# The first two rows of a spectral gate and token mixer: second root on ScalarE straight from the variance, first weights' low part on GpSimd, low part of row 0 in two halves

## The chip, the cores and the metric

The kernel runs on one core of a Trainium2 chip. The metric is the device time of one execution in microseconds (us). Before the change it is 366.05 us, the median of 3 runs (365.9 to 366.07).

## The reference

The input x has 2048 tokens of 512 channels. It is layer-normalised over the channels. One branch multiplies its two-dimensional Fourier transform by a filter and transforms back. The other branch normalises again, mixes over the tokens with two matrix products and a GELU between them, and goes through a SiLU. The output is x plus the product of the two.

```python
def _layernorm(x, axis=-1, eps=1e-5):
    m = jnp.mean(x, axis=axis, keepdims=True)
    v = jnp.var(x, axis=axis, keepdims=True)
    return (x - m) / jnp.sqrt(v + eps)

X = rfft2(xn) * (w_r + 1j * w_i)                       # A
s = irfft2(X, s=(S, D))
h = _layernorm(xn)                                     # B
u = gelu(einsum("bsd,sf->bdf", h, w1) + b1)            # F = 1792
y = einsum("bdf,fs->bds", u, w2) + b2
out = x + s * silu(transpose(y))                       # xn = _layernorm(x)
```

With v the variance of a token of x, the first layer norm scales by 1/sqrt(v + eps), and both together by 1/sqrt(v(1 + eps) + eps^2). So a token needs two inverse roots of the same variance.

## The kernel before, in words

**Tiling.** The 2048 tokens are 16 "rows" j of 128 tokens (one to a partition) by 512 channels. The first product accumulates over the 16 rows in PSUM: for each j, a weight tile of 128 x 128 by the row's 128 x 512. A product of two fp32 numbers is made of three products in the fp32r format: each operand is split into a high part (a rounded copy, made by `high` on ScalarE) and a low part (the number minus its high part, made by `low` on VectorE), and the products are high x high, low x high and high x low. For the weights the tiles are `w[a][0]` (high, named w1h in the trace) and `w[a][1]` (low, w1l), where a is 0 or 1 for the two halves of the columns (3 x 128 = 384 columns each in this first stage). For the data they are `hh[j]` and `hl[j]`, and the normalised row before the split is `h`; all three bear the name h in the trace. In the trace these matmuls stand under line 139, as every operation that is recorded through the helper class `Kept`.

**Order.** Nearly all instructions of the first stage are wrapped in `keep`, which fixes the order of the program on each engine's queue; the rest is ordered by the planner of the language from its costs. Each engine works its queue in order and waits at semaphores for what other engines make.

**The first rows.** To start TensorE early, rows 0 and 1 have steps of their own, which this change touches.

- `issued` (lines 449 to 452) sends the first transfers in pieces from two queues at a time: row 0 of x, the first half of the weights of row 0, row 1 of x, the second half of the weights; GpSimd's queue waits for row 0 of x (a one-column copy, line 457) and then issues more.
- TensorE first multiplies zeros (`wz`, line 443), and then twice the first high weights by themselves (lines 487 and 488).
- `stats` and `first_roots` (lines 218 to 224): mean and variance with bn_stats and bn_aggr, both sums v2 = (v + eps, v(1 + eps) + eps^2) on VectorE, both roots in one ScalarE instruction (sd), and on VectorE t = -v2/2.
- `first_scales` (lines 226 to 237): the reciprocal r0 of both roots, and one Newton step for each. The second one (index b) is done on VectorE (lines 229 and 230), as hh waits for it. The first one (index a) is done on GpSimd by four small instructions (lines 231 to 234), and then two more give q, the ratio of the two scales (`product_of_scales`, lines 240 and 241), with which `turned` (line 280) scales the small Fourier table cf for the other branch. `between` makes hh of row 0 directly on VectorE (`normed_v`, line 272, two halves of 256 channels); after it comes nb, minus mean times scale (line 237).
- `normed` (line 268) makes h on ScalarE from nb and the scale, also in two halves of 256 channels. The halves lie interleaved in the tile in blocks of 128 channels (`mirrored`).
- `low(w[0][1], ...)` is the first low part of the weights and `low(hl[0], h, hh[0])` the low part of row 0, both on VectorE, line 469.

TensorE takes for row 0, in this order, groups of 3 matmuls: first high weights x hh, second high weights x hh, first low weights x hh, first high weights x hl, second high weights x hl, second low weights x hh. After row 0 each row takes the full 18 matmuls, and on odd rows the first transform of the Fourier branch between them. Later stages (filters, the rest of the first product, the second product, the gate) are not touched.

Of the kernel before, what the change touches and what calls it, by code (L numbers as in the profile page):

```python
# [9 lines left out]
F32 = mybir.dt.float32  # L10
F32R = mybir.dt.float32r
AF = mybir.ActivationFunctionType
ALU = mybir.AluOpType
PSUM = bass.MemoryType.PSUM

P = 128
# [3 lines left out]
EPS = 1e-5  # L20
# [121 lines left out]
def spectral_mixer_kernel(tc, x, w1, b1, w2, b2, wk, we, wx, c_f, c_ft, c_d, c_i, c_g, c_h, out):  # L142
    nc = tc.nc
    V, A, G, T, SY = nc.vector, nc.scalar, nc.gpsimd, nc.tensor, nc.sync

    def pool(stack, side, name, bufs):
        return stack.enter_context(tc.tile_pool(name=name, bufs=bufs, side=side, reuse_waits="tile"))


    def mirrored(t, turned):  # L150
        v = t.rearrange("p (h q c) -> p h q c", q=2, c=P)
        return v[:, :, 0], v[:, :, 1, ::-1] if turned else v[:, :, 1]
# [9 lines left out]
    with tc.tile_pool(name="ps", bufs=1, space=PSUM) as psp, ExitStack() as left, ExitStack() as right:  # L162
# [25 lines left out]
        lnp = pool(rstage, "right", "ln", 2)  # L188
        hs = [new_hu(f"h{j}") for j in range(NJ)]
        hh, hl = [h[:, 0] for h in hs], [h[:, 1] for h in hs]  # L190
        xs = {}
# [8 lines left out]
        def x_pair(k):  # L200
            t = lnp.tile([P, 2, D], F32, name=f"x{k}", tag="x", bufs=3)
            xs.update({2 * k: t[:, 0], 2 * k + 1: t[:, 1]})
            return t
# [4 lines left out]
        keep = tc.keep_in_program_order  # L208

        def moments(nm, n):  # L210

            return {k: lnp.tile([P, 2, w], F32, name=f"{k}{nm}", tag="m" + k, bufs=3)[:, :n]
                    for k, w in (("st", 6), ("mv", 2), ("v2", 2), ("sd", 2), ("r0", 2), ("t", 2), ("rs", 2), ("nb", 1),
                                 ("q", 1))}

        def first_roots(m):
            var = m["mv"][:, 0, 1:2]
            keep(V.bn_aggr(m["mv"][:, 0], m["st"][:, 0]))  # L220
            keep(V.tensor_scalar(m["v2"][:, 0, 1:2], var, 1.0 + EPS, EPS * EPS, op0=ALU.mult, op1=ALU.add))
            keep(V.tensor_scalar(m["v2"][:, 0, 0:1], var, EPS, None, op0=ALU.add))
            keep(A.activation(m["sd"], m["v2"], AF.Sqrt))
            keep(V.tensor_scalar(m["t"], m["v2"], -0.5, None, op0=ALU.mult))

        def first_scales(m, between=lambda: None):
            (ta, tb), (ra, rb), (sa, sb) = ([m[n][:, 0, k:k + 1] for k in range(2)] for n in ("t", "r0", "rs"))
            keep(V.reciprocal(m["r0"], m["sd"]))
            keep(V.scalar_tensor_tensor(tb, rb, rb, tb, op0=ALU.mult, op1=ALU.mult))
            keep(V.scalar_tensor_tensor(sb, tb, 1.5, rb, op0=ALU.add, op1=ALU.mult))  # L230
            keep(G.tensor_mul(ta, ta, ra))
            keep(G.tensor_mul(ta, ta, ra))
            keep(G.tensor_scalar(ta, ta, 1.5, None, op0=ALU.add))
            keep(G.tensor_mul(sa, ta, ra))
            product_of_scales(m)
            between()
            keep(V.scalar_tensor_tensor(m["nb"], m["mv"][:, :, 0:1], -1.0, m["rs"][:, :, 1:2], op0=ALU.mult, op1=ALU.mult))

        def product_of_scales(m):
            keep(G.tensor_mul(m["q"], m["rs"][:, :, 0:1], m["rs"][:, :, 1:2]))  # L240
            keep(G.tensor_mul(m["q"], m["q"], m["v2"][:, :, 1:2]))

        def stats(m, i, src):
            keep(V.bn_stats(m["st"][:, i], src))
# [25 lines left out]
        def normed_v(dst, src, m, i, k):  # L270
            for to, v in zip(mirrored(dst, False), mirrored(src, True)):
                keep(V.tensor_scalar(to, v, m["mv"][:, i, 0:1], m["rs"][:, i, k:k + 1], op0=ALU.subtract, op1=ALU.mult))

        def new_h(j):
            return lnp.tile([P, D], F32, name=f"h{j}", tag="h", bufs=3)
# [49 lines left out]
        def w1_tiles(j):  # L325
            return [[w1r.tile([P, NE1 * P], F32R, name=f"w1{n}{a}_{j}", tag=f"w1{n}{a}", bufs=3) for n in "hl"] for a in range(2)]
# [114 lines left out]

        wz = lnp.tile([P, D // 2], F32R, name="wz", tag="t")
        G.memset(wz.bitcast(F32), 0.0)
        raws = {}
        x_pair(0)
        w1_pair(0)
# [8 lines left out]
        m = moments("m0", 1)  # L455
# [9 lines left out]
        def high(dst, src):  # L465
            keep(A.activation(dst, src, AF.Copy))  # L466

        def low(dst, src, hi):
            keep(V.tensor_sub(dst, src, hi.bitcast(F32)))  # L469
# [11 lines left out]

        stats(m, 0, xs[0])
        first_roots(m)
        w = w1_tiles(0)
        h = new_h(0)
        high(w[0][0], raws[0, 0])
        for _ in range(WARM // 4):
            T.matmul(ps[:, 0, :P], w[0][0][:, :P], w[0][0][:, :P], start=True, stop=True)
        first_scales(m, lambda: normed_v(hh[0], xs[0], m, 0, 1))
        high(w[1][0], raws[0, 1])  # L490
        normed(h, xs[0], m, 0)
        m1 = moments("m1", 1)
        stats(m1, 0, xs[1])
        low(w[0][1], raws[0, 0], w[0][0])
        first_roots(m1)
        low(hl[0], h, hh[0])
        first_scales(m1)
        low(w[1][1], raws[0, 1], w[1][0])
        of = {0: (m, 0), 1: (m1, 0)}
        m = moments("m2", 2)  # L500
# [7 lines left out]
        for j in range(NJ):  # L508
# [26 lines left out]
            if more:  # L535
                w = w1_tiles(j + 1)
                h = new_h(j + 1)
# [35 lines left out]
            if more:  # L573
# [10 lines left out]
                if j % 2 == 0 and j + 4 < NJ:  # L584
                    m = moments(f"m{j + 4}", 2)
# [199 lines left out]
        for n in range(8):  # L785
            a, b, c, d, e, f = PACE[n]
            u, v, w = ([None] * (k < MADE[n]) for k in range(3))
# [128 lines left out]
        def copied(name, src, where):  # L916
            t = where.tile([P, HD], F32, name=name, tag=name.split("_")[0], bufs=1)
            step(A.activation(t, src, AF.Copy))
            return t
# [17 lines left out]
        V, A, SY, G = (Kept(e, keep) for e in (nc.vector, nc.scalar, nc.sync, nc.gpsimd))  # L937
# [113 lines left out]
        for p in range(NP):  # L1051
# [8 lines left out]
            for k, n in enumerate(ORDER):  # L1060
# [7 lines left out]
                elif n == 6:  # L1068
                    v2 = copied(f"v2_{p}", bx, fp)
# [77 lines left out]
```

## Time and profile before

| | |
|---|---|
| Runs | 366.05 us median (365.9 to 366.07) |
| Profiled execution, its own time | 366.06 us |
| Its span, first to last instruction | 364.3 us |
| Mean granted TensorE clock | 0.999 |
| Busy: TensorE / weight loads | 357.9 us (98%) / 310.6 us (85%) |
| Busy: VectorE / ScalarE / GpSimd | 305.9 (84%) / 211.2 (58%) / 87.1 us (24%) |
| Busy from 0 to 7 us: TensorE / VectorE / ScalarE / GpSimd | 5.27 / 2.58 / 2.01 / 3.70 us |
| Busy from 7 to 13 us: TensorE / VectorE / ScalarE / GpSimd | 5.96 / 5.65 / 4.85 / 2.13 us |

The profile is of one execution. PE is TensorE's matmuls, PEld its weight loads, DVE is VectorE, ACT ScalarE, POOL GpSimd. A timeline row gives start and duration in us, engine, line of the kernel, operation, output<-input by the names of the program, the shape, the count of merged instructions, and in brackets how long the engine had been idle and what ended that. Neighbouring instructions of one kind are merged into a row; instructions of one engine overlap a little, since the next one starts while the last is finishing. The ends of matmuls are modelled.

### The profile page before, as it was taken

How to read it: one execution, taken by the hardware profiler on the slowest of the kernel's cores; microseconds unless marked ns; L12 is line 12 of the kernel's file. 1: busy time of each engine (PE TensorE's matmuls, PEld its weight loads, DVE VectorE, ACT ScalarE, POOL GpSimd, SP SyncE). 2: the span in 40 equal slices, each digit the busy share in tenths (PEclk: the TensorE clock that was granted, in tenths of full speed). 3: DMA queues.
4: the chain of work that ended last, by engine and by line, in shares of the span. 5: the costliest groups of instructions: out<-in, count | busy, mean ns of one | idle time of the engine just before them, and what ended most of it. 6: DMA issues, size and time to landing. Idle time of an engine off the chain costs nothing.

```text
span 364.3 us, 8799 instructions
## 1 busy us (share of the span) xinstructions
PE 357.9 (98%) x3452; PEld 310.6 (85%) x3452; DVE 305.9 (84%) x587; ACT 211.2 (58%) x385; POOL 87.1 (24%) x134
## 2 busy tenths in 40 slices
PE   8999999999999999999999999999999999999994
PEld 7788888888777778777888999989898989898983
DVE  4899999967799996999995988687887969696984
ACT  3887788857534426755237875555464546565441
POOL 4233333323222012220111001040403223140330
PEclk9999999999999999999999999999999999999999
DMA  7978999306695596896568288688888989897724
GB/s 211 245 188 199 218 279 315 160 0 161 184 237 202 190 261 177 244 241 199 175 222 171 101 228 176 187 175 204 185 187 211 172 231 158 233 161 216 124 28 89
DMA packets 33293, 68.66 MB, mean 188 GB/s; under 512 B 4612, under 2 KB 19380, under 8 KB 33124
## 3 DMA queue, kind: packets, MB, share of 16 engines
q1 hardware_dynamic: 24276, 42.44, 42.0%
q0 software_dynamic: 8496, 25.01, 32.2%
q10 hardware_dynamic: 480, 0.66, 0.6%
q8 instruction: 27, 0.44, 0.5%
q14 instruction: 14, 0.11, 0.1%
HBM read 59.70 MB, written 8.13 MB: 186 GB/s over the span
## 4 chain that ended last, share of the span: by engine, by line
PE 97%; DMA 1%; ACT 0%; DVE 0%; ACTq 0%; issue 0%; DVEq 0%
PE ps L139 97%; DMA w1r<-in_w_dram 1%; DVE rows L139 0%; ACTq L452 0%; ACT w1h L466 0%; ACT g L139 0%; DVEq L1143 0%
## 5 line engine op out<-in xcount | busy, mean ns | idle before, releaser
L139 PE MATMUL ps<-h,w1h 128*128 128x512 f32 x400 | 116.5, 398 | 0.0
L139 PEld LDWEIGHTS ps<-h,w1h 128*128 128x128 f32 x400 | 72.9, 188 | 19.9 <-issue 4.9
L139 PE MATMUL ps<-h,w1l 128*128 128x512 f32 x200 | 67.6, 390 | 0.0
L139 DVE TENSOR_TENSOR w2f<-a,w2f 128x896 fp32r<-128x896 f32 x36 | 39.2, 1090 | 21.6 <-ACT w2f L139 21.6
L139 PEld LDWEIGHTS ps<-h,w1l 128*128 128x128 f32 x200 | 37.6, 188 | 8.1
L139 ACT ACTIVATE w2f<-a 128x896 fp32r<-128x896 f32 x36 | 36.8, 1023 | 12.8 <-PE ps L139 7.5
L139 PE MATMUL ps<-fb,w2f 128*128 128x256 f32 x336 | 41.9, 280 | 0.0
L139 POOL DMA_DIRECT2D s<-in_w_dram x14 | 18.4, 1311 | 96.1 <-DVE c L139 46.4
L139 PE MATMUL ps<-fa,w2f 128*128 128x256 f32 x336 | 41.3, 278 | 0.0
L139 PEld LDWEIGHTS ps<-fb,w2f 128*128 128x128 f32 x336 | 39.7, 188 | 0.9 <-issue 0.8
L139 PE MATMUL ps<-fc,w2f 128*128 128x256 f32 x336 | 39.9, 278 | 0.0
L139 PEld LDWEIGHTS ps<-fa,w2f 128*128 128x128 f32 x336 | 39.8, 188 | 0.0
L139 PEld LDWEIGHTS ps<-fc,w2f 128*128 128x128 f32 x336 | 39.2, 188 | 0.0
L139 POOL DMA_DIRECT2D out_dram<-r x28 | 23.6, 1278 | 27.5 <-DVE r L139 27.5
L155 ACT ACTIVATE w1h<-w1s 128x512 fp32r<-128x512 f32 x26 | 16.2, 632 | 23.7 <-PE ps L139 11.7
L667 POOL DMA_DIRECT2D xc<-xc x16 | 9.8, 620 | 70.3 <-ACT xc L665 55.1
L308 POOL TENSOR_TENSOR ey<-t 128x256 f32<-128x256 f32 x16 | 15.7, 978 | 44.0 <-DVE t L306 44.0
L139 ACT ACTIVATE w2f<-s 128x896 fp32r<-128x896 f32 x15 | 15.3, 1023 | 13.8 <-PE ps L139 12.4
L469 DVE TENSOR_TENSOR w1l<-w1r,w1h 128x384 fp32r<-128x384 f32 x32 | 21.3, 670 | 0.0
L139 PE MATMUL ps<-fd,w2f 128*128 128x256 f32 x168 | 20.7, 278 | 0.0
L139 ACT ACTIVATE g<-c,b2t 128x256 f32<-128x256 f32 x24 | 12.1, 505 | 14.6 <-DVE c L139 14.6
L268 ACT ACTIVATE h<-x,nbm,rsm 128x256 f32<-128x256 f32 (+1 forms) x34 | 18.4, 591 | 3.6 <-DVE nbm L263 3.0
(134 smaller groups left out, 605.7 us busy)
## 6 DMA issues: line engine op xcount, KB each, us to landing
a<-in_w_dram SPq DMA_DIRECT2D x22, 448.0 KB, 4.1
wt<-in_wk_dram POOLq DMA_DIRECT2D x16, 512.0 KB, 5.9
s<-in_w_dram SPq DMA_DIRECT2D x16, 448.0 KB, 4.5
s<-in_w_dram POOLq DMA_DIRECT2D x16, 448.0 KB, 6.8
w1s<-in_w_dram SPq DMA_DIRECT2D x52, 128.0 KB, 5.0
w1r<-in_w_dram SPq DMA_DIRECT2D x28, 192.0 KB, 4.7
xc<-xc POOLq DMA_DIRECT2D x16, 256.0 KB, 3.0
out_dram<-in_x_dram SPq DMA_DIRECT2D x4, 960.0 KB, 6.5
```

Of the source, the lines that this page charges most:

```text
L139: return lambda *args, **kw: self.keep(operation(*args, **kw))
L155: return A.activation(hi, src, AF.Copy), V.tensor_sub(lo, src, hi.bitcast(F32))
L268: keep(A.activation(to, v, AF.Identity, bias=m["nb"][:, i], scale=m["rs"][:, i, 1:2]))
L308: G.tensor_add(ey[:, 0::3, :, j], a, b)
L469: keep(V.tensor_sub(dst, src, hi.bitcast(F32)))
L667: keep(G.dma_start(*(v.rearrange("p s t c -> p s (t c)") for v in (there[c::2], here[1 - c::2, ::-1]))))
```

## The change: what it does

Four edits, all within the steps for rows 0 and 1.

1. Roots: the second root is taken by ScalarE straight from the variance, as sqrt((1 + eps) v + eps^2) with scale and bias in the instruction, ahead of the two VectorE sums. The bias is a new one-column tile `tiny`, set by GpSimd behind `wz`. The first root is a ScalarE instruction of its own.
2. Scales: the reciprocals are taken one by one. On VectorE the order is now: reciprocal b, t = -v2/2, the two Newton instructions of b, `between`, nb, reciprocal a. Then `meanwhile`, then the GpSimd instructions of a and q.
3. The first low part of the weights of row 0 is made by GpSimd, in `meanwhile`, ahead of its small instructions. It is no longer made by VectorE.
4. The low part of row 0 is made by two VectorE instructions of 256 channels, one for each of the halves that `normed` writes.

Both rows take edits 1 and 2; edits 3 and 4 are for row 0 alone.

```diff
         def first_roots(m):
             var = m["mv"][:, 0, 1:2]
             keep(V.bn_aggr(m["mv"][:, 0], m["st"][:, 0]))
+            keep(A.activation(m["sd"][:, 0, 1:2], var, AF.Sqrt, bias=tiny, scale=1.0 + EPS))
             keep(V.tensor_scalar(m["v2"][:, 0, 1:2], var, 1.0 + EPS, EPS * EPS, op0=ALU.mult, op1=ALU.add))
             keep(V.tensor_scalar(m["v2"][:, 0, 0:1], var, EPS, None, op0=ALU.add))
-            keep(A.activation(m["sd"], m["v2"], AF.Sqrt))
+            keep(A.activation(m["sd"][:, 0, 0:1], m["v2"][:, 0, 0:1], AF.Sqrt))
+
+        def first_scales(m, between=lambda: None, meanwhile=lambda: None):
+            (ta, tb), (ra, rb), (sa, sb), (da, db) = ([m[n][:, 0, k:k + 1] for k in range(2)] for n in ("t", "r0", "rs", "sd"))
+            keep(V.reciprocal(rb, db))
             keep(V.tensor_scalar(m["t"], m["v2"], -0.5, None, op0=ALU.mult))
-
-        def first_scales(m, between=lambda: None):
-            (ta, tb), (ra, rb), (sa, sb) = ([m[n][:, 0, k:k + 1] for k in range(2)] for n in ("t", "r0", "rs"))
-            keep(V.reciprocal(m["r0"], m["sd"]))
             keep(V.scalar_tensor_tensor(tb, rb, rb, tb, op0=ALU.mult, op1=ALU.mult))
             keep(V.scalar_tensor_tensor(sb, tb, 1.5, rb, op0=ALU.add, op1=ALU.mult))
+            between()
+            keep(V.scalar_tensor_tensor(m["nb"], m["mv"][:, :, 0:1], -1.0, m["rs"][:, :, 1:2], op0=ALU.mult, op1=ALU.mult))
+            keep(V.reciprocal(ra, da))
+            meanwhile()
             keep(G.tensor_mul(ta, ta, ra))
...
             product_of_scales(m)
-            between()
-            keep(V.scalar_tensor_tensor(m["nb"], m["mv"][:, :, 0:1], -1.0, m["rs"][:, :, 1:2], op0=ALU.mult, op1=ALU.mult))
...
+        tiny = lnp.tile([P, 1], F32, name="tiny", tag="tiny")
+        G.memset(tiny, EPS * EPS)
...
-        first_scales(m, lambda: normed_v(hh[0], xs[0], m, 0, 1))
+        first_scales(m, lambda: normed_v(hh[0], xs[0], m, 0, 1),
+                     lambda: keep(G.tensor_sub(w[0][1], raws[0, 0], w[0][0].bitcast(F32))))
         high(w[1][0], raws[0, 1])
         normed(h, xs[0], m, 0)
         m1 = moments("m1", 1)
         stats(m1, 0, xs[1])
-        low(w[0][1], raws[0, 0], w[0][0])
         first_roots(m1)
-        low(hl[0], h, hh[0])
+        for to, src, hi in zip(*(mirrored(t, False) for t in (hl[0], h, hh[0].bitcast(F32)))):
+            keep(V.tensor_sub(to, src, hi))
         first_scales(m1)
         low(w[1][1], raws[0, 1], w[1][0])
```

## The prediction

> **What bounds the kernel now.** I read the chain of waits first, for which engine carries the span.
>
> ```profile
> core 0 of [0], span 364.3 us
> ...
> 9.55 350.15 PE ps L139 x3415
> ```
>
> From 9.55 us on it is one unbroken run of matmuls to within a few microseconds of the end. So a microsecond is worth a microsecond only if TensorE starts that run sooner, and the change, which touches the first two rows alone, can act only on what lies before it. Next I read the timeline of the matmuls and that of the weight loads around this point. Columns: start, duration, engine, line, operation, count, and in brackets the idle time before and what ended it.
>
> ```profile
> 8.66 0.86 PE L139 MATMUL ps<-h,w1l 128*128 128x512 f32 x3
> 9.55 1.66 PE L139 MATMUL ps<-h,w1h 128*128 128x512 f32 x6
> 11.05 0.84 PE L139 MATMUL ps<-h,w1l 128*128 128x512 f32 x3
> 11.73 0.84 PE L139 MATMUL ps<-h,w1h 128*128 128x512 f32 x3
> ```
> ```profile
> 7.84 0.53 PEld L139 LDWEIGHTS ps<-h,w1h 128*128 128x128 f32 x3 [0.27 <-ACT w1h L466]
> 8.43 0.66 PEld L139 LDWEIGHTS ps<-h,w1l 128*128 128x128 f32 x3
> 9.55 1.23 PEld L139 LDWEIGHTS ps<-h,w1h 128*128 128x128 f32 x6 [0.47 <-DVE h L469]
> 10.82 0.65 PEld L139 LDWEIGHTS ps<-h,w1l 128*128 128x128 f32 x3
> ```
>
> Unhindered groups give the cadence: three matmuls from 11.05 to 11.73, so 0.227 us each. The group of 8.66 could have been followed at 8.66 + 3 x 0.227 = 9.34. Counted back from 11.05, the six with hl began in effect at 11.05 - 6 x 0.227 = 9.69, which is 0.14 after their first weight load was let go at 9.55. So this stall costs 9.69 - 9.34 = 0.35 us, and it is put down to the VectorE subtraction that makes hl of row 0. It is the last stall before the unbroken run: 0.35 us is all that the change can win here. The other wait in these rows, at 7.84, is for the high part of the second half of the weights, on ScalarE.
>
> What comes before hl is in VectorE's and ScalarE's timelines:
>
> ```profile
> 4.88 0.18 DVE L220 BATCH_NORM_AGGREGATE mvm<-stm 128x2 f32<-128x6 f32 x1
> 5.10 0.15 DVE L221 TENSOR_SCALAR v2m<-mvm 128x1 f32<-128x1 f32 x1
> 5.17 0.14 DVE L222 TENSOR_SCALAR v2m<-mvm 128x1 f32<-128x1 f32 x1
> 5.34 0.17 DVE L224 TENSOR_SCALAR tm<-v2m 128x2 f32<-128x2 f32 x1
> 5.58 0.17 DVE L228 RECIPROCAL r0m<-sdm 128x2 f32<-128x2 f32 x1
> 5.78 0.24 DVE L229 SCALAR_TENSOR_TENSOR tm<-r0m,tm 128x1 f32<-128x1 f32 x1
> 6.06 0.16 DVE L230 SCALAR_TENSOR_TENSOR rsm<-tm,r0m 128x1 f32<-128x1 f32 x1
> 6.25 0.74 DVE L272 TENSOR_SCALAR h<-x,mvm,rsm 128x256 fp32r<-128x256 f32 x2
> 6.90 0.15 DVE L237 SCALAR_TENSOR_TENSOR nbm<-mvm,rsm 128x1 f32<-128x1 f32 x1
> 6.97 0.69 DVE L244 BATCH_NORM_STATS2 stm<-x 128x6 f32<-128x512 f32 x1
> 7.58 0.54 DVE L469 TENSOR_TENSOR w1l<-w1r,w1h 128x384 fp32r<-128x384 f32 x1
> 8.03 0.18 DVE L220 BATCH_NORM_AGGREGATE mvm<-stm 128x2 f32<-128x6 f32 x1
> ...
> 8.81 0.69 DVE L469 TENSOR_TENSOR h<-h,h 128x512 fp32r<-128x512 f32 x1
> 9.41 0.16 DVE L228 RECIPROCAL r0m<-sdm 128x2 f32<-128x2 f32 x1
> ...
> 10.08 0.16 DVE L237 SCALAR_TENSOR_TENSOR nbm<-mvm,rsm 128x1 f32<-128x1 f32 x1
> 10.16 1.03 DVE L469 TENSOR_TENSOR w1l<-w1r,w1h 128x384 fp32r<-128x384 f32 x2
> ```
> ```profile
> 5.34 0.20 ACT L223 ACTIVATE sdm<-v2m 128x2 f32<-128x2 f32 x1 [0.53 <-DVE v2m L222]
> 6.18 0.52 ACT L466 ACTIVATE w1h<-w1r 128x384 fp32r<-128x384 f32 x1 [0.64 <-DMA w1r<-in_w_dram]
> 7.26 0.53 ACT L466 ACTIVATE w1h<-w1r 128x384 fp32r<-128x384 f32 x1 [0.56 <-DMA w1r<-in_w_dram]
> 7.70 1.08 ACT L268 ACTIVATE h<-x,nbm,rsm 128x256 f32<-128x256 f32 x2
> ```
>
> hl (8.81) needs both halves of h, which ScalarE writes from 7.70 to 8.78. ScalarE starts them as soon as it is through with the weights' copy of 7.26, and that one waited for a transfer. So the start of h is set by a DMA, which the change leaves alone.
>
> **The change, part by part.** Root straight from the variance: now the root starts at 5.34, 0.03 after the second small VectorE step ended (5.31). It would start after the aggregation, 5.06 + 0.03 = 5.09, and end at 5.29. The reciprocal follows 0.04 later (as 5.58 follows 5.54): 5.33. The multiplication by -0.5, hidden beside ScalarE at 5.34 today, now stands behind the reciprocal: it starts 0.07 after it (the spacing of 5.10 and 5.17), at 5.40, and ends at 5.57. The two Newton steps follow with today's gaps, 5.60 and 5.88; hh of row 0 runs from 6.07 to 6.81 instead of 6.25 to 6.99, and nb starts at 6.72 instead of 6.90. That is 0.18 us sooner, but on the path it buys nothing: the first three matmuls come sooner, the next three still wait for the weights of 7.84, and h on ScalarE starts no earlier than 7.70. The added second root on ScalarE (0.20) lies in its idle 0.64 before 6.18. The added constant is a one-column memset on GpSimd, microseconds before the root that reads it; cost nothing; if it were late, the root would be late with it, with the 0.18 as its slack.
>
> Low part of the first weights on GpSimd: VectorE loses the 0.54 of 7.58. Second-row statistics, 0.18 sooner and directly behind nb and one more reciprocal (0.07 of spacing), run 6.86 to 7.55, the aggregation from 7.59, and the two small steps end 0.43 later (5.31 - 4.88), at 8.02. On GpSimd the subtraction starts when ScalarE's copy ends, 6.70, plus the 0.09 that GpSimd takes to start behind VectorE in the rows below (20.23 to 20.32), so at about 6.79. No subtraction of 384 columns on GpSimd is in the trace. The nearest is L308, 256 columns:
>
> ```profile
> 19.82 0.41 DVE L306 TENSOR_TENSOR t<-zt 128x256 f32<-128x256 f32 x1
> 20.27 0.43 DVE L309 TENSOR_TENSOR ey<-t 128x256 f32<-128x256 f32 x1
> ...
> 20.82 0.50 DVE L259 TENSOR_TENSOR tm<-r0m 128x4 f32<-128x4 f32 x1
> ```
> ```profile
> 20.32 0.98 POOL L308 TENSOR_TENSOR ey<-t 128x256 f32<-128x256 f32 x1 [5.41 <-DVE t L306]
> ```
>
> Upper end: 0.98 x 384/256 = 1.47. Lower end: VectorE's addition of the same inputs ends at 20.70, and if GpSimd got on only then, its own work was 21.30 - 20.70 = 0.60, or 0.90 for 384. That VectorE's multiplication of four columns at 20.82 lasted 0.50 and ended at 21.32, just behind GpSimd's 21.30, says that the two do hold each other off, so I take 0.90. Started at 6.79 and held off by nb till 6.87, it ends at 7.77; at 1.47 it ends at 8.34. TensorE wants this part for the load of 8.43, and 0.1 later would still do, since a load need be only 0.14 ahead of its matmul. The cover is the six matmuls with the high parts; were it gone, every 0.1 us past 8.53 would cost 0.1.
>
> [...]
>
> GpSimd's own small steps stand behind the subtraction:
>
> ```profile
> L231 POOL TENSOR_TENSOR tm<-tm,r0m 128x1 f32<-128x1 f32 x2 | 0.4, 202 | 2.2 <-DVE r0m L228 2.1
> 12.27 0.57 ACT L280 ACTIVATE cf<-cf,qm 128x64 f32<-128x64 f32 x2
> ```
>
> At 0.20 each and a gap of 0.08, as between VectorE's dependent steps or a little more, the first row's six end at 7.77 + 6 x 0.28 = 9.45. Their product is first read by the copies at 12.27, and 2.8 us of slack hide the delay. The second row's six start behind its moved reciprocal, at about 10.2, and meet VectorE's two subtractions of 10.05 to 11.1; if these let only two of them through, four more end at 11.1 + 4 x 0.28 = 12.2, just ahead of the second copy. That is a cover of about 0.1 to 0.3 us, and what goes over it TensorE's next small matmuls would wait for.
>
> hl in two halves: the first half of h is ready at about 7.70 + 1.08/2 + 0.04 = 8.28, the second at 8.78. VectorE is free from 8.02, so the first half runs from 8.3 for 0.42 (L309 is as wide, 0.43) and the second from 8.81 to 9.24. TensorE's load goes at 9.29 instead of 9.55 (the same 0.05 behind hl as now), the matmuls in effect at 9.43 instead of 9.69: 0.26 us gained, 0.09 of the stall left. Halving without the offload would give less: VectorE would only then be through with the weights and the roots.
>
> What is late next: the low part of the second half of the weights. In the new order behind 9.24 stand the reciprocal (9.15, as 9.41 stands to 9.50), the -0.5 step (0.07), the rest as now up to nb at 9.89, one more reciprocal (0.08), and the subtraction at 10.05, which ends at 10.59; TensorE can load it at 10.64. With the gain it wants that load no later than 9.43 + 6 x 0.227 - 0.14 = 10.65. It just fits; I take off 0.01 for it. The second row's normalised values follow nb, which moves by 0.19, and keep their distance to TensorE.
>
> **Sum.** -0.25 us: the profiled execution's own 366.06 becomes 365.8; it lies 0.01 above the median of the runs, so the same number stands for both. In share it is 0.07%, under the 0.2% (0.73 us) that a measurement of this kernel can tell from no change.
>
> **Rivals.** (1) GpSimd gets to the data first and holds nb off (slower). nb reads two arrays, as the subtraction does, and is due at 6.72, GpSimd at 6.79: a lead of 0.07. If the roots come 0.07 later than worked out, nb waits for the whole subtraction, as the step of 20.82 did. With 0.90 nb runs from 7.69 to 7.84, h on ScalarE starts at 7.88, 0.18 late, and its second half ends at 8.96. VectorE, held up too, is through with statistics, aggregation and small steps at 7.84 + 0.69 + 0.04 + 0.43 = 9.00; the first half of hl runs from 8.92, the second from 9.26 to 9.68, and the load is at 9.73: 0.18 us later than today, 366.25. With 1.47 the same steps lie 0.57 further back: 0.75 slower, 366.8. It decides from the moment that nb starts after GpSimd. For it: 20.82; against it: the lead, and the small width of nb. [...] Chance 0.22, of it 0.05 for the far end.
>
> (2) The halves don't come apart: the halves of h lie interleaved, and if the first subtraction were made to wait for both, hl would run 8.81 to 9.24 and 9.15 to 9.57, 0.07 later than now: 366.13. Against it: L308 and L309 write interleaved parts of one tile and start 0.05 apart. Chance 0.06.
>
> (3) The gain is eaten again by the low part of the second weights or by GpSimd's late product: 366.05. For it: that part fits with 0.01 only, the product with 0.1 to 0.3; against it: a miss of 0.1 costs 0.1, not the whole. Chance 0.12.
>
> (4) Something outside the first rows moves, because the planner of the program sets another order in later stages; no row prices it. Chance 0.04, of it 0.03 faster by over 0.2%.
>
> **The numbers.** The forecast has the remaining 0.56. From the best case (the whole 0.35: 365.7) to rival 1 at 0.90 (366.25), with 0.15 on either side for the spread of the runs (365.9 to 366.07), the range is 365.55 to 366.4. Faster by over 0.2%: 0.03. Slower by over 0.2%: 0.06 (the far end of rival 1 and 0.01 of rival 4). Within: 0.91.
>
> **What would show it.** Root: the reciprocal of row 0 at about 5.33, hh ending near 6.81, and yet the weight load still near 7.84. Offload: the GpSimd subtraction of 0.9 from about 6.8, and the aggregation of row 1 near 7.6. Halves: two VectorE subtractions of 0.42, the second ending near 9.24, and the load that waits for hl near 9.29. Wrong if nb ends behind the GpSimd subtraction (rival 1), if the first half starts only after 8.78 (rival 2), or if a new wait stands before the loads of 10.6 or the copies of cf (rival 3).

## The result, and the profile after

| | before | after |
|---|---|---|
| Median of 5 runs each | 366.05 us (365.8 to 366.7) | 369.42 us (368.33 to 370.49) |
| Profiled execution, its own time | 366.06 us | 369.56 us |
| Its span | 364.3 us | 367.7 us |
| Mean granted TensorE clock, profiled execution | 0.999 | 0.995 |

After over before is 1.009, with a 95% interval of 1.0074 to 1.0106. The forecast was 365.8 us, a change too small to be told from none; the kernel became 3.4 us slower and lies 3.6 us above the forecast, six times the distance from the forecast to the top of the range. So the question is not which term was a little off, but what was not in the sum at all.

The place is easy to find. The chain of waits of the changed kernel still has the unbroken run of matmuls, but it begins at another time, and it is cut once:

```profile
8.97 194.51 PE ps L139 x1876
...
213.73 5.32 DMA a<-in_w_dram
...
222.03 141.10 PE ps L139 x1378
```

A convenient mark for the end of the head is the first matmul of the Fourier transform that follows row 0: at 13.18 us before, at 16.24 after, 3.06 later. The cut at 222 us adds 0.36 more; the experiments come back to it. Now the head, engine by engine, first the timelines of ScalarE and VectorE of the changed kernel (start, duration, engine, line, operation, idle time before and what ended it):

```profile
5.27 1.28 ACT L221 ACT_TABLE_LOAD   x1 [5.27 <-DVE mvm L220]
6.56 0.29 ACT L221 ACTIVATE sdm<-mvm,tiny 128x1 f32<-128x1 f32 x1
6.76 0.19 ACT L224 ACTIVATE sdm<-v2m 128x1 f32<-128x1 f32 x1
6.86 0.92 ACT L471 ACTIVATE w1h<-w1r 128x384 fp32r<-128x384 f32 x2
```
```profile
5.00 0.18 DVE L220 BATCH_NORM_AGGREGATE mvm<-stm 128x2 f32<-128x6 f32 x1
...
6.89 0.17 DVE L228 RECIPROCAL r0m<-sdm 128x1 f32<-128x1 f32 x1 [1.46 <-ACT sdm L221]
...
7.61 1.31 DVE L275 TENSOR_SCALAR h<-x,mvm,rsm 128x256 fp32r<-128x256 f32 x2
8.83 0.15 DVE L233 SCALAR_TENSOR_TENSOR nbm<-mvm,rsm 128x1 f32<-128x1 f32 x1
...
10.03 0.76 DVE L502 TENSOR_TENSOR h<-h,h 128x256 fp32r<-128x256 f32 x2
```

Two things were not forecast. The first row of ScalarE is no arithmetic: it is a table load (ACT_TABLE_LOAD) that stands on the line of the square root, 1.28 us long, *after* the variance is there. In the kernel before, the same load stood far ahead of the root:

```profile
3.53 1.28 ACT L223 ACT_TABLE_LOAD   x1 [3.53 <-issue]
```

The second is hh at 7.61: the two instructions take 1.31 where they took 0.74. GpSimd's timeline has its subtraction across them:

```profile
7.45 0.99 POOL L495 TENSOR_TENSOR w1l<-w1r,w1h 128x384 fp32r<-128x384 f32 x1 [1.45 <-ACT w1h L471]
```

TensorE then waits twice, 0.89 and 1.11 us, and what it does next takes much longer than its numbers of matmuls warrant:

```profile
7.42 0.44 PE L139 MATMUL ps<-w1h 128*128 128x128 f32 x2 [0.89 <-ACT w1h L471]
8.97 2.59 PE L139 MATMUL ps<-h,w1h 128*128 128x512 f32 x6 [1.11 <-DVE h L275]
11.36 1.48 PE L139 MATMUL ps<-h,w1l 128*128 128x512 f32 x3
12.64 1.63 PE L139 MATMUL ps<-h,w1h 128*128 128x512 f32 x6
```

Six matmuls take 2.59 at 8.97 and 1.63 at 12.64. The table by stretches says why. Its columns are the window, its length, the busy time of PE, PEld, DVE, ACT and POOL with their numbers of instructions, the granted TensorE clock, and the DMA share and rate. After, then before:

```profile
5.00:9.00 4.00, 2.00 (x13) 1.72 (x12) 2.40 (x12) 2.50 (x5) 1.99 (x3) 1.00 0.90 281
9.00:12.00 3.00, 3.00 (x8) 2.38 (x9) 2.83 (x14) 2.18 (x6) 1.57 (x7) 0.57 1.04 253
12.00:14.00 2.00, 2.00 (x8) 1.59 (x8) 1.98 (x6) 2.00 (x6) 1.32 (x6) 0.80 1.02 250
```
```profile
5.00:9.00 4.00, 3.36 (x20) 2.71 (x20) 3.55 (x17) 2.33 (x6) 2.07 (x8) 1.00 0.95 291
9.00:12.00 3.00, 2.96 (x14) 2.11 (x13) 2.90 (x9) 2.25 (x5) 1.72 (x6) 1.00 1.10 247
```

From 5 to 9 us TensorE worked 2.00 us of 4 after the change, and 3.36 before. In the 5 us behind that the granted clock is 0.57 and 0.80: 3 x 0.43 + 2 x 0.20 = 1.7 us of full speed lost. In stretches of half a microsecond the same view shows 0.50 in each from 9.5 to 12.5 us and 0.90 and 0.69 in the two beside them: about 3.4 us at half clock. Busy time alone hides this: TensorE shows 3.00 of 3.00 in the stretch in which it does little more than half the work (8 matmuls for 14).

Added up, from the profiled executions: x lands 0.12 later (statistics at 4.27 instead of 4.15, which the change does not touch); the root starts 1.22 later, so 1.10 of it is the change; from the start of the root to the end of hh it takes 0.71 longer, of which 0.57 is hh and 0.09 the slower root; from there to the transform it takes 1.13 longer, which is the lost clock of 1.7 less the stalls that vanished (0.48 of them: in e1 below, which keeps its clock, this stretch is 5.71 us and in the kernel before 6.19). 0.12 + 1.10 + 0.71 + 1.13 = 3.06. With the 0.36 at 222 us the matmuls end 3.42 later.

### The profile page after: what moved, and what is told of

Its sections match the earlier page's. It is cut to its first block, busy times and chain, and to the rows that moved or that the text cites. A ratio compares the mean times of both kernels' runs of the same rounds, so it can differ in the third digit from the quotient of the medians.

```text
span 367.7 us, 8806 instructions
## 1 busy us (share of the span) xinstructions
PE 359.6 (98%) x3452; PEld 312.1 (85%) x3452; DVE 305.2 (83%) x589; ACT 210.5 (57%) x387; POOL 87.5 (24%) x136
## 4 chain that ended last, share of the span: by engine, by line
PE 91%; DVE 3%; DMA 2%; ACT 1%; issue 1%; DVEq 0%; ACTq 0%; SPq 0%
PE ps L139 91%; DMA a<-in_w_dram 1%; DMA x<-in_x_dram 1%; DVE a L842 1%; ACT fc L366 0%; ACT w2f L139 0%; DVE w2f L830 0%; ACT w2f L826 0%; DVE c L139 0%; DVE rows L139 0%; DVE stm L247 0%; ACT u L358 0%; DVE fc L371 0%; DVE fa L371 0%; ACT L221 0%
## 5 line engine op out<-in xcount | busy, mean ns | idle before, releaser
L139 PEld LDWEIGHTS ps<-h,w1h 128*128 128x128 f32 x400 | 73.7, 190 | 20.9 <-issue 4.9
L474 DVE TENSOR_TENSOR w1l<-w1r,w1h 128x384 fp32r<-128x384 f32 x31 | 20.2, 657 | 1.0 <-ACT w1h L471 0.7
```

The source lines that it names most:

```text
L139: return lambda *args, **kw: self.keep(operation(*args, **kw))
```

## The experiments

The theory at this point had three parts: the first root waits for two engines, and that moves the table load behind the variance (the second wait, for short); GpSimd's subtraction holds VectorE's hh off (the lock); and TensorE's waits cost it the clock. The rivals were that the load went along with the new form of the root whatever it waits for; that hh is slow for another reason (another order, the transfers); and that the clock fell by chance. The recorded expectations call the first part theory W, the second G or L, and the third C; theory P is that the planner set another order in later stages, theory D that the clock costs nothing. Each experiment is given with its ratio to the kernel before, run beside it on the same chip (365.83 to 366.01 us there), and the 95% interval.

ScalarE's queue in the built program, with its waits, shows how the second wait acts (shortened). The last lines are the kernel before, the first ones the kernel after; DVE_49 is the variance or its sum, Pool_49 the constant.

```
5 L221 ACT_TABLE_LOAD [waits DVE_49]
6 L221 ACTIVATE sdm_117<-mvm_115,tiny 128x1 [waits Pool_49]
...
5 L223 ACT_TABLE_LOAD
6 L223 ACTIVATE sdm_115<-v2m_114 128x2 [waits DVE_49]
```

In the kernel before, the root carries its one wait itself, and the load ahead of it waits for nothing: it starts at 3.53. In the kernel after, only the wait for the constant stays with the root; the wait for the variance stands ahead of the load, which starts at 5.27. The trace of the kernel after has a small instruction there, EVENT_SEMAPHORE, of 17 ns on the root's line; that of the kernel before has none on its root's line. In the chains of waits the step stands on the root's line just ahead of the load, 0.02 us long, at 5.22 in the kernel after, 5.00 in e2 and 5.30 in e4; that of e1 has none on that line. The line in the kernel after (count, duration in ns, first and last start):

```profile
L221 ACTq EVENT_SEMAPHORE  x1: 17/17/17, 5.2 to 5.2; - x1
L221 ACT ACT_TABLE_LOAD  x1: 1283/1283/1283, 5.3 to 5.3; - x1
```

**e1: the constant made by VectorE.** The kernel after, with one wait less.

```diff
-        G.memset(tiny, EPS * EPS)
+        V.memset(tiny, EPS * EPS)
```

> The changed kernel whole, with the constant of the first root set by VectorE instead of GpSimd, so that this root waits for one engine and not for two. Theory W (the table load got the first of two waits, and stands behind the variance): the load is back near 3.5, the root of row 0 starts near 5.1, hh is ready near 6.8, TensorE has no long gap and keeps its clock; 365.8, or 366.25 if nb is held off by GpSimd. Theory G (GpSimd's subtraction holding VectorE off is what costs): 368 or more, as now. Theory P (the planner's order of later stages): about 369, the head alone better.

Measured: 366.23 us, 1.0011 [1.0001, 1.002]. Of the 0.9% some 0.8 are gone, 2.9 us. ScalarE's timeline has the load back at its early place, and the root where the forecast had it (5.09):

```profile
3.53 1.28 ACT L221 ACT_TABLE_LOAD   x1 [3.53 <-issue]
5.07 0.29 ACT L221 ACTIVATE sdm<-mvm,tiny 128x1 f32<-128x1 f32 x1 [0.25 <-DVE mvm L220]
```

So the second wait moves the load, not the new form of the root. The time is that of the expectation's second branch (366.25, nb held off), but by another instruction: nb is not what is held. hh still is, beside the same GpSimd instruction (VectorE's timeline, then GpSimd's):

```profile
6.11 1.42 DVE L275 TENSOR_SCALAR h<-x,mvm,rsm 128x256 fp32r<-128x256 f32 x2
```
```profile
6.34 1.04 POOL L495 TENSOR_TENSOR w1l<-w1r,w1h 128x384 fp32r<-128x384 f32 x1 [0.49 <-ACT w1h L471]
```

**e2: edits 1 and 2 alone**, the constant left on GpSimd, both low parts as before.

```diff
-        first_scales(m, lambda: normed_v(hh[0], xs[0], m, 0, 1),
-                     lambda: keep(G.tensor_sub(w[0][1], raws[0, 0], w[0][0].bitcast(F32))))
+        first_scales(m, lambda: normed_v(hh[0], xs[0], m, 0, 1))
...
+        low(w[0][1], raws[0, 0], w[0][0])
...
-        for to, src, hi in zip(*(mirrored(t, False) for t in (hl[0], h, hh[0].bitcast(F32)))):
-            keep(V.tensor_sub(to, src, hi))
+        low(hl[0], h, hh[0])
```

> Edits 1 and 2 alone (roots and scales), constant on GpSimd; the low part of the first weights and of row 0 as before. Theory W: the load starts only behind the variance, near 5.2, the root near 6.5, hh ends near 8.4; with some loss of TensorE's clock 367.5 to 369. Theory G: 366.0, since nothing is on GpSimd.

Measured: 367.36 us, 1.006 [1.0037, 1.0084]. The load is late again, hh is not held. Four of the 7 runs, at a mean granted clock of 0.999 or more, took 366.77 to 367.36; the other three, at 0.988 to 0.997, took 368.47 to 369.62.

```profile
5.05 1.28 ACT L221 ACT_TABLE_LOAD   x1 [5.05 <-DVE mvm L220]
```
```profile
7.39 0.73 DVE L275 TENSOR_SCALAR h<-x,mvm,rsm 128x256 fp32r<-128x256 f32 x2
```

**e3: edits 3 and 4 alone**, with the old roots and scales.

```diff
-            keep(A.activation(m["sd"][:, 0, 1:2], var, AF.Sqrt, bias=tiny, scale=1.0 + EPS))
-            keep(A.activation(m["sd"][:, 0, 0:1], m["v2"][:, 0, 0:1], AF.Sqrt))
+            keep(A.activation(m["sd"], m["v2"], AF.Sqrt))
...
-            keep(V.reciprocal(rb, db))
+            keep(V.reciprocal(m["r0"], m["sd"]))
...
-            keep(V.reciprocal(ra, da))
```

> Edits 3 and 4 alone (subtraction on GpSimd, low part of row 0 in halves), roots as before. Theory W: no delay of the load; nb, due at 6.90, comes after GpSimd's start near 6.79 and is held off to about 7.8, so 366.25; 365.8 if it isn't held off. Theory G: 367.5 or more.

Measured: 366.47 us, 1.0028 [1.0013, 1.0042]. hh held for 1.57 without any late load, so the lock is a cost of its own (VectorE's timeline, then GpSimd's, then the two instructions of hh by line with minimum, median and maximum in ns):

```profile
6.30 1.57 DVE L273 TENSOR_SCALAR h<-x,mvm,rsm 128x256 fp32r<-128x256 f32 x2
```
```profile
6.40 0.99 POOL L491 TENSOR_TENSOR w1l<-w1r,w1h 128x384 fp32r<-128x384 f32 x1 [0.45 <-ACT w1h L467]
```
```profile
L273 DVE TENSOR_SCALAR h<-x,mvm,rsm x2: 402/822/1243, 6.3 to 7.5; 128x256 fp32r<-128x256 f32 x2
```

One instruction is as long as ever (402), the other 0.84 longer. Here the runs fall apart: 8 of 12, with mean granted clocks of 0.997 or more, took 365.93 to 366.58; the other 4, at 0.992 to 0.995, took 367.47 to 368.3. TensorE's waits in the head are shorter here in sum (0.26 and 1.12 us in the trace), and whether they cost the clock differs from run to run. The instruction expected to be held was nb; it was hh.

**e4: the second wait put into the kernel before**, and nothing else: a column of zeros, set by GpSimd, as the bias of the old root.

```diff
+        nil = lnp.tile([P, 1], F32, name="nil", tag="nil")
+        G.memset(nil, 0.0)
...
-            keep(A.activation(m["sd"], m["v2"], AF.Sqrt))
+            keep(A.activation(m["sd"], m["v2"], AF.Sqrt, bias=nil))
```

> The kernel before with one thing added: the bias of its first root is a column of zeros that GpSimd sets in the first microsecond, so that the root waits for two engines. The value is unchanged. Theory W: the table load stands behind the sums of 5.31 and the root starts near 6.6, 1.25 later than before: 367.3 to 368.7. Theories G and P: 366.05, no change.

Measured: 368.5 us, 1.0069 [1.0054, 1.0084]. With the work of the kernel before, the second wait alone moves the load from 3.53 to 5.35 and costs 2.5 us:

```profile
5.35 1.28 ACT L223 ACT_TABLE_LOAD   x1 [5.35 <-DVE v2m L222]
6.64 0.29 ACT L223 ACTIVATE sdm<-v2m,nil 128x2 f32<-128x2 f32 x1
```

The root is 1.30 later; the rest goes with the clock, as far as one run can show: five of six runs at 0.995 or less took 368.38 to 368.89, the one at 1.0 took 367.23.

**e5: TensorE kept busy.** The kernel after with 7 more multiplications of zeros and 10 more of the first weights by themselves; they fill the time in which TensorE would wait.

```diff
-        for moving in [wz] * (2 * WARM + 4) + [wz[:, :P]] * 6:
+        for moving in [wz] * (2 * WARM + 4) + [wz[:, :P]] * 13:
...
-        for _ in range(WARM // 4):
+        for _ in range(WARM // 4 + 10):
```

> The changed kernel as it is, with seventeen more matmuls on dummy data that keep TensorE busy while it waits for the first weights and for hh. Theory C (of the 3.4 us that the change costs, about 1.6 is TensorE's granted clock falling to half for some 3.4 us after the long wait): no slice of the head below full clock, 367.7 or so, 1.6 faster than the changed kernel. Theory D (the delay of hh is all, the clock costs nothing): 369.4, no change.

Measured: 367.45 us, 1.0041 [1.0026, 1.0057], against 1.009 for the kernel after: 0.0049 x 366 = 1.8 us come back with more work and the same late load and held hh. By stretches:

```profile
5.00:9.00 4.00, 4.00 (x30) 3.77 (x30) 2.44 (x11) 2.69 (x6) 1.86 (x4) 1.00 0.93 288
9.00:12.00 3.00, 3.00 (x14) 2.49 (x14) 2.83 (x14) 2.19 (x7) 1.64 (x7) 1.00 1.08 265
```

The clock stays at 1.00, 14 matmuls are done from 9 to 12 instead of 8, and the transform starts at 14.40 instead of 16.24, 1.84 sooner, of which 0.21 is x, which landed sooner (statistics at 4.06, not 4.27). So the waits cost the clock, and its share comes out alike three ways: 1.8 us in time, 1.6 in the head, 1.7 by the granted clock. No single idle time of TensorE in the head of the kernel after was longer than 1.11 us, so the clock fell without a longer one. In the profiled executions the clock fell to half for about 3.4 us where TensorE had worked 1.95 to 2.63 us of the 4 from 5 to 9 (after, e3, e4, e13, e14), and did not where it had worked 3.01 or more; as the runs of one kernel differ (e2, e3, e4), that is no sharp bound. What makes the clock fall, and why for 3.4 us, the runs do not show.

**e6: the change without its offload**, the constant on VectorE: edits 1, 2 and 4, the first low part back on VectorE. And **e12**, the same once more.

```diff
-        G.memset(tiny, EPS * EPS)
+        V.memset(tiny, EPS * EPS)
...
-        first_scales(m, lambda: normed_v(hh[0], xs[0], m, 0, 1),
-                     lambda: keep(G.tensor_sub(w[0][1], raws[0, 0], w[0][0].bitcast(F32))))
+        first_scales(m, lambda: normed_v(hh[0], xs[0], m, 0, 1))
...
+        low(w[0][1], raws[0, 0], w[0][0])
```

> Constant by VectorE, roots and halves as in the change, the first weights' low part back on VectorE. Theory L (GpSimd's subtraction holds off VectorE's making of hh): hh ends near 6.85 and takes 0.74 again; VectorE is through with the weights by 8.5, the second half of hl is ready near 9.25 all the same, and the stall before the hl matmuls is gone: 365.65 beside 365.9 for the kernel before. If GpSimd isn't what held hh: as e1, 0.3 above the kernel before.

> The kernel of e6 once more, to narrow its interval: 0.25 to 0.4 faster than the kernel before, the stall before the hl matmuls gone.

Measured: 365.71 us, 0.9993 [0.9983, 1.0003], and 365.79 us, 1.0001 [0.9992, 1.0009]. This is the forecast's head, without GpSimd. VectorE and the weight loads of e6:

```profile
6.09 0.74 DVE L275 TENSOR_SCALAR h<-x,mvm,rsm 128x256 fp32r<-128x256 f32 x2
...
8.27 0.75 DVE L502 TENSOR_TENSOR h<-h,h 128x256 fp32r<-128x256 f32 x2
```
```profile
8.30 0.65 PEld L139 LDWEIGHTS ps<-h,w1l 128*128 128x128 f32 x3
9.08 1.26 PEld L139 LDWEIGHTS ps<-h,w1h 128*128 128x128 f32 x6
```

No wait stands before hl's load at 9.08; in e12 it is at 9.23, behind a wait of 0.28. From the statistics to the transform it takes 8.67 us in e6 and 9.03 in the kernel before: 0.36 won in the head, and not to be seen in the time. The 0.25 to 0.4 us that e12 was to confirm did not appear: its median is 0.1 below the kernel before.

**e7: the change whole, with GpSimd made to wait for hh.** The constant on VectorE, and ahead of GpSimd's subtraction a copy of one column of hh on GpSimd.

```diff
+        def low_on_pool():
+            keep(G.tensor_copy(m["q"][:, 0], hh[0][:, D - 1:].bitcast(F32)))
+            keep(G.tensor_sub(w[0][1], raws[0, 0], w[0][0].bitcast(F32)))
```

> Constant by VectorE and the whole change, with one thing more: a one-column copy of hh on GpSimd ahead of its subtraction, so that this starts only when hh is made. Theory L: hh takes 0.74, the subtraction runs from about 7.1 to 8.1 and is in time for 8.43, nothing with weight is held off; 365.65. If the offload itself is too slow or holds off something else: as e1 or slower.

Measured: 365.69 us, 0.9992 [0.9981, 1.0002]. VectorE's hh and GpSimd's subtraction no longer overlap, and hh has its old length:

```profile
6.10 0.73 DVE L275 TENSOR_SCALAR h<-x,mvm,rsm 128x256 fp32r<-128x256 f32 x2
```
```profile
7.20 1.01 POOL L496 TENSOR_TENSOR w1l<-w1r,w1h 128x384 fp32r<-128x384 f32 x1
```

e1 and e7 differ by the order alone (and the small copy that sets it): 1.0011 against 0.9992 is 0.7 us in time, with intervals that all but touch, so the size is rough; the head shows 0.5 (from the statistics to the transform 9.12 us in e1 and 8.60 in e7). That is what holding hh off costs where the clock is kept. e6 and e7 differ by the offload and agree in time: placed so, the offload brings nothing.

**e8, e11, e13, e14: which property of hh lets GpSimd hold it off?** The lock's part of the theory leaves open whether it is the width of the instruction or the columns (mean and scale for each partition) that it reads beside x. e8 is e1, and e11 is e3, with fixed numbers in place of the columns; what they compute as hh is not the normalised row.

```diff
-                keep(V.tensor_scalar(to, v, m["mv"][:, i, 0:1], m["rs"][:, i, k:k + 1], op0=ALU.subtract, op1=ALU.mult))
+                keep(V.tensor_scalar(to, v, 0.0, 20.0, op0=ALU.subtract, op1=ALU.mult))
```

> The kernel of e1, but hh is made by the same VectorE instruction with two fixed numbers in place of the two columns from memory (so hh isn't the normalised row). If it is the columns that make this instruction meet GpSimd's subtraction, both halves now take 0.41 while the subtraction runs; if it is the wide input, one half takes about 1.0 to 1.2 again.

> The kernel of e3, but hh is made with two fixed numbers in place of the two columns (so hh isn't the normalised row), and at about the time at which GpSimd's subtraction starts. If only the columns make the instruction meet GpSimd: 0.285 for each half, whatever GpSimd does. If the wide input does: one half takes about 1 us again.

Measured: 365.78 us, 0.9992 [0.9973, 1.001], and 365.39 us in a single execution. Neither decides: with numbers the instructions take 0.285 instead of 0.41, and were through, or all but through, when GpSimd began (e8: hh from 5.91 to 6.40, GpSimd at 6.48). But e8 shows who is *not* held (VectorE, then GpSimd):

```profile
6.47 0.69 DVE L247 BATCH_NORM_STATS2 stm<-x 128x6 f32<-128x512 f32 x1
```
```profile
6.48 1.00 POOL L495 TENSOR_TENSOR w1l<-w1r,w1h 128x384 fp32r<-128x384 f32 x1 [0.69 <-ACT w1h L471]
```

The statistics read 512 columns right beside the subtraction and take their usual 0.69. To force the overlap, e13 puts the numbers into the kernel after, whose late root lets GpSimd come first; e14 puts a number in for the mean alone, and keeps the scale's column. In both hh is not the normalised row. The edit of e14:

```diff
-                keep(V.tensor_scalar(to, v, m["mv"][:, i, 0:1], m["rs"][:, i, k:k + 1], op0=ALU.subtract, op1=ALU.mult))
+                keep(V.tensor_scalar(to, v, 0.0, m["rs"][:, i, k:k + 1], op0=ALU.subtract, op1=ALU.mult))
```

> The changed kernel, with hh made from two fixed numbers in place of the two columns (so hh isn't the normalised row); here the late root puts it surely beside GpSimd's subtraction. Columns theory (the columns are what makes it wait for GpSimd): both halves 0.285, done while the subtraction still runs. Width theory (any wide instruction of this kind on VectorE waits): one half lasts about 0.9 to 1.0, till the subtraction is over.

> The same with one column (the scale) and one fixed number (so hh isn't the normalised row). Columns theory: one half lasts about 1.0 as in the changed kernel if one column is enough, 0.3 to 0.4 if it takes two. Width theory: about 1.0.

Measured: 368.98 and 368.86 us, one execution each, of which the trace is what counts. The two instructions of hh by line in e13, and then in e14:

```profile
L275 DVE TENSOR_SCALAR h<-x x2: 280/692/1105, 7.3 to 8.4; 128x256 fp32r<-128x256 f32 x2
```
```profile
L275 DVE TENSOR_SCALAR h<-x,rsm x2: 341/662/983, 7.4 to 8.3; 128x256 fp32r<-128x256 f32 x2
```

The one that meets GpSimd is held until its subtraction is over, with numbers too: in e13 it starts at 7.33, takes 1.105 and ends at 8.43, beside a subtraction from 7.29 to 8.28; in e14 it starts at 7.39, takes 0.983 and ends at 8.37, beside one from 7.24 to 8.23. So it is not the columns: this instruction, with one input and one output of 256 channels, was held in all three forms (0.98 to 1.24), and the statistics, 512 wide, were not (0.69 in e8 and e11). What sets the two apart the runs do not show. Over all runs: hh is held in the seven in which it overlaps the subtraction by more than 0.1 us (after, e1, e3, e5, e10, e13, e14) and in no other.

**e9: edit 4 alone** on the kernel before.

```diff
-        low(hl[0], h, hh[0])
+        for to, src, hi in zip(*(mirrored(t, False) for t in (hl[0], h, hh[0].bitcast(F32)))):
+            keep(V.tensor_sub(to, src, hi))
```

> The kernel before with edit 4 alone (low part of row 0 in halves). By the prediction's steps: VectorE is through with the weights and the sums near 8.6, so the first half runs to about 9.0 and the second to about 9.35, 0.15 sooner than the whole one; 0.1 to 0.15 faster than the kernel before. If the halves didn't come apart: 0.07 slower.

Measured: 365.92 us, 1.0001 [0.9993, 1.001]. The halves, and the load that waits for them:

```profile
8.61 0.75 DVE L497 TENSOR_TENSOR h<-h,h 128x256 fp32r<-128x256 f32 x2
```
```profile
9.41 0.76 PEld L139 LDWEIGHTS ps<-h,w1h 128*128 128x128 f32 x4 [0.42 <-DVE h L497]
```

From the aggregation of row 0 to the transform it takes 0.16 us less than before (13.06 - 4.92 against 13.18 - 4.88); the time does not show it.

**e10: another cure for the load.** The kernel after, the constant on GpSimd, and ahead of it all a root of the constant that nobody reads, so that the load belongs to an instruction with one wait.

```diff
+        scratch = lnp.tile([P, 1], F32, name="scratch", tag="scratch")
+        keep(A.activation(scratch, tiny, AF.Sqrt))
```

> The changed kernel, with a root of the constant taken into an unused column ahead of all, so that the table is loaded by it. Theory W: load near 3.5, root of row 0 near 5.1, the rest as in e1 (hh held off by GpSimd): 366.2 to 366.5. If it is something else in the new root that delays it: 369 as now.

Measured: 366.2 us, 1.0024 [1.0003, 1.0044]. The load is early again and belongs to the unread root; the real one starts at 4.99. It need not wait for the constant any more, though: the unread root, at 4.83, has already read it, and the chain of waits has no such step as EVENT_SEMAPHORE on the real one's line. So e10 shows the cure, not that a root with two waits is free. hh is held as in e1:

```profile
3.54 1.28 ACT L461 ACT_TABLE_LOAD   x1 [3.54 <-issue]
...
4.99 0.29 ACT L221 ACTIVATE sdm<-mvm,tiny 128x1 f32<-128x1 f32 x1
```
```profile
6.03 1.52 DVE L275 TENSOR_SCALAR h<-x,mvm,rsm 128x256 fp32r<-128x256 f32 x2
```

Nine of the 12 runs, at clocks of 0.997 or more, took 365.97 to 366.37, two at 0.995 took 367.08 and 367.72. The profiled one took 370.6, with a granted clock of 0.95 from 7 us to the end, another thing than the 3.4 us at half clock, and unexplained; the rows above are of ScalarE and VectorE alone.

**The 0.36 at 222 us.** From the first transform to the start of the last 21 matmuls it takes 343.86 us before (357.04 - 13.18), 344.22 in the kernel after and 344.28 in e1, but 343.82 to 343.87 in e2 to e9, e11, e12 and e14, and 343.98 in e13. The wait for VectorE at 222.03, of 0.38, stands in e1 and e7 as well (0.34 and 0.35), in e7 without any loss over the whole stretch. e5, e13 and e14 have both the late load and the offload. So it goes neither with the late load nor with the offload as such; whether it is of these single executions or of the change stays open.

## Why the prediction was wrong, point by point

- **What bounds the kernel: right.** The unbroken run of matmuls decides, and nothing outside the head moved that the experiments could tie to the change. That 0.35 us was all there was to win held to within 0.1: e6 and e7 won 0.36 and 0.43 in the head, the second weights having come somewhat sooner as well (copied from 6.67 and 7.07, not 7.26).
- **"It would start after the aggregation, 5.06 + 0.03 = 5.09": this step failed.** The root's own data was ready at 5.18, and it started at 6.56. The step took for granted that the table load of 3.53 stays where it is, and that row was not even among the rows read: it is no operation of the source, so no line of the diff moves it. In e1, where the load stays, the root starts at 5.07.
- **"The added constant is a one-column memset on GpSimd ... cost nothing": this is where it broke.** The memset itself (0.10 us at 1.0 in the kernel after) was not seen to cost anything: e10 keeps it on GpSimd, and nine of its 12 runs took 365.97 to 366.37, where e1 has 366.23. The semaphore that the root now waits for in addition is what pushed the other wait ahead of the load (5.27 instead of 3.53; 5.35 in e4). The prediction asked only whether the constant would be late. Price: e4, 2.5 us, 1.30 of it directly and the rest, as its one run at full clock says, by the clock.
- **Rival 1: right mechanism, wrong victim.** GpSimd does hold VectorE off, and for the whole subtraction: the instruction that met it took 1.09 us in e1 and 1.24 in e3 instead of 0.41. The prediction looked for the instruction with two input arrays, nb; the one that was held is hh, with one array and two columns. nb, one column wide, only came late behind it. The prediction also had GpSimd at 6.79, since ScalarE's first copy stood at 6.18; in e1 and e3 it began at 6.34 and 6.40, within hh. The order that the sum needed was thus as much a matter of when a transfer lands as of the change. Price: 0.5 us in the head and 0.7 in time (e1 against e7), where the rival had 0.18 to 0.75.
- **The clock was in no term.** The prediction priced each late step at its own lateness. From 5 to 9 us TensorE did 1.36 us less work than before (2.00 against 3.36), and that cost 1.7 us on top. This is the largest term of the 3.4, and it follows from the late root and the held hh; where these are cured or TensorE is kept busy (e1, e5, e7), it is gone.
- **Terms that held.** GpSimd's subtraction: 0.99, between the bounds 0.90 and 1.47, though the lower end had been taken; it started 0.08 behind ScalarE's copy (forecast 0.09). The halves came apart, so rival 2 fell: 0.42 each, the second ending at 9.02 in e6 (forecast 9.24). The load of hl: 9.08 in e6, e7 and 9.23 in e12 (forecast 9.29). That such a gain can't be told from no change: right for e6, e7 and e12.
- **A term that was not there to be won.** The offload of 0.54 us from VectorE was costed as what lets the halves start early. e6 has the low part on VectorE and loads hl at the same 9.08 as e7: the earlier roots and the halves do it.

## What to carry to other kernels

Before adding an operand to an instruction, look at what the queue holds ahead of it that it brought along (here the table load), and count the engines that it would wait for: make a constant on the engine that makes the other operand (e1, the load at 3.53), or give the load an instruction of its own with one wait (e10, 3.54). Work moved to GpSimd must be placed in time against VectorE's wide instructions, those of one input too, or tied behind them (e7), for here hh did not end until GpSimd's 0.99 us were over. And price a wait of TensorE's not by its length alone: where the busy time of 4 us falls to a half, look at the granted clock of the 5 us behind (here 2.00 us of work, then 0.57 and 0.80).

## What the hardware showed that was not expected

- The 1.28 us load stands behind the first of two waits: where the root waits for one engine, the load starts at 3.53 or 3.54 (before, e1, e3, e6 to e9, e11, e12), where for two, at 5.05 to 5.35 (after, e2, e4, e5, e13, e14).
- A granted clock of 0.57 after 2.00 us of work in 4; no single idle time was longer than 1.11 us. About 3.4 us at half clock in the trace; a mean clock of 0.995 or less, with 1 us or more lost, in 5 of 6 runs of e4 and in 4 of 12 of e3.
- VectorE's 128x256 instruction of hh takes 0.285 us with two numbers, 0.34 with one column and 0.41 with two, and is held by GpSimd's subtraction in each of these forms (0.98 to 1.24). VectorE ahead by 0.10 was still held (e3, 6.30 to 6.40), ahead by 0.23 it was not, but the next instruction was (e1, 6.11 to 6.34). The statistics, 512 wide, were not held beside it (0.68 to 0.69 in e7, e8, e11).
- A root of one column takes 0.28 to 0.30 us with its bias from a column (line 221 in after, e1, e2), 0.18 to 0.20 without (line 224 there); of two columns 0.29 (e4) and 0.20 (before).
